# Sums of weight tiles and weight blocks as adding transfers from GpSimd's queue, in a delta-rule attention followed by a gated FFN

## The chip, the cores and the metric

The kernel runs on one core of one Trainium2 chip. The metric is the device time of one execution in microseconds (us), as a median over runs. A profile is one execution taken by the hardware profiler; it times every instruction on the five engines: PE (TensorE, the matrix engine; PEld is its weight load), DVE (VectorE), ACT (ScalarE), POOL (GpSimd) and SP (SyncE), and the transfers of the 16 DMA engines.

## The reference

The inputs are q, k and v of 4 batches x 8 heads x 768 steps x 48 columns and beta, all float32, and three weight matrices (gate and val 384 x 1536, out 1536 x 384), which are float64, and a gain of 384.

```python
k_n = k / (norm(k) + 1e-06)
for t in range(S):                      # state: 48 x 48 per batch and head, from zero
    y[:, :, t] = einsum('bhd,bhde->bhe', q[:, :, t], state)
    v_old = einsum('bhde,bhd->bhe', state, kt)
    state = state + bt * einsum('bhd,bhe->bhde', kt, vt - v_old)
x = y.transpose(0, 2, 1, 3).reshape(3072, 384)
xn = x / sqrt(mean(x * x) + 1e-06) * rms_g
g = xn @ w_gate
out = (g * sigmoid(g) * (xn @ w_val)) @ w_out
```

## The kernel before, in words

The sequence is cut into 12 chunks of 64 steps (NCH = 12). Of each chunk, `prep` builds what does not depend on the state: the transposed keys, the products of keys with keys (L532), and by a recursion of DVE steps (L693, a product, and L699, a sum, 15 of each per chunk) the inverse of a triangular 64 x 64 matrix per head, assembled from 32-step halves through DRAM (`dkk`, `dx`, `dxt`) and two merges on PE (L775, L799). For chunks 0 and 1 the products with beta at its start (L646, L671, L676) run on DVE, for later ones on POOL. `recur` then applies the state: `on_state` (L840) multiplies the transposed keys and queries with it, L886 and L900 give the corrected values and the output, `ku` (L1019) and a sum on DVE (L1028) update the state. Keys and state are padded from 48 to 64 rows per head (`DP`), so that two heads lie in the two halves of the 128 partitions; pairs of 64-row halves and 64-column halves of PE are used side by side. The output of a chunk (256 tokens x 384) is normed, transposed and scaled into `xf` (or `xp1` for chunk 1).

The FFN of chunks 0 and 1 (`ffn_plain`) multiplies directly: 12 column blocks of 128, each an `up` (L1064: gate and val), silu on ACT (L1071), a product on DVE (L1072) and a `down` (L1046). Its first half uses blocks 0 to 5 (half 0 of the weights) of chunk 0 and then chunk 1, its second half blocks 6 to 11 (half 1). The FFN of chunks 2 to 11 (`ffn`) uses fewer block products: 15 products per half of the weights (L1157) of sums of the input blocks with sums of the weight blocks, and a similar scheme in `down` (L1214). A `more_` product is added into `tmp` on DVE (L1167), another is copied by ACT (L1169).

The weights come as 64-bit floats in 18 tiles of 768 KB, in the order of `weights`: per half, pairs of gate and val for three input column groups, with the three tiles of `w_out` in between (tiles 4, 7, 8 and 13, 16, 17). A tile is loaded into one of three `raw` buffers (parts of `more`) and converted with integer steps: ACT makes the scaled high word (L460), DVE shifts it (L448), masks it into a scratch tile `cc` (L451) and multiplies the low word in (L456), and the sum of both is written into `w_in` or `wo_sb` (L480). `cc` is one of two buffers, `tmp` for even tiles and a part of `more` for odd ones. Tiles 0 to 2 are summed on PE (L472, L473), all others on DVE.

`factors(h)` makes the sums of weight blocks of half h for `ffn`: six into `extra[h]`, which lies where the raw buffers and the odd `cc` were, and two in place in `w_in`, once the plain FFN has read that half (the key `wuse`). They are 13 DVE instructions per half (L1120, L1122), each 128 x 512. `out_factors` (L1193) does the like for `w_out`.

No engine decides at run time: a list scheduler in the file (`Plan`) takes each step's engine, estimated duration, dependencies and priority, with due times for some transfers (`after`), simulates 60 rounds with a random shake from a seed, and emits the best order found, which every engine then follows in its own queue. Padding matmuls (`filler`, L1312) are put into planned gaps of PE in the first 70 us of the plan.

Of the kernel before, what the change touches and what calls it, by code (L numbers as in the profile page):

```python
# [59 lines left out]
class Plan:  # L60
# [150 lines left out]
    def run(self, free, filler=None, until=0.0):  # L211
        self.first_priorities()
        best = None
        self.ends = []
        rng = random.Random(19)
        for k in range(ROUNDS):
            order = self.forward([t for t, _ in free], until if filler else 0.0)
            if order is None:
                break
            self.ends.append(self.end)  # L220
            if best is None or self.end < best[0]:
                best = self.end, [(op, op.start) for op in order]
            self.backward()
            for op in self.ops:
                op.key += SHAKE * (k % 3) * rng.uniform(-1.0, 1.0)
        self.end = best[0]
        pe = 0.0
        free = list(free)
        for op, s in best[1]:
            op.start = s  # L230
            for g in op.acquire:
                if g.t is None:
                    g.t = free.pop(0)[1]
            if filler and op.eng == "PE":
# [12 lines left out]
def kernel(  # L247
# [113 lines left out]
    def dma(dst, src, prio, r=(), w=(), work=0.3, dur=0.5, eng="SP", after=0.0):  # L361
        queue = nc.scalar if eng == "ACT" else nc.sync
        op = P.add(eng, dur, lambda: queue.dma_start(out=dst, in_=src), prio, r, w, lat=0.7)
        op.dma, op.work, op.ready = True, work, after

    PERIOD = 51.0

    def due(c, lead):
# [51 lines left out]
    def weights():  # L420
        todo = []
        for half_ in range(2):
            c0 = half_ * WCOL

            for i_ in range(3):
                for side, (key, w) in enumerate((("wg", moe_w_gate), ("wv", moe_w_val))):
                    c1 = c0 + 256 * i_
                    src = w.rearrange("(t p) c -> p t c", p=128)[:, :, c1 : c1 + 256]
                    todo.append((w_in[:, side, half_, i_:9:3], src, [(key, half_, i_)]))
                if i_:  # L430
                    for f in ((6 * half_,) if i_ == 1 else (6 * half_ + 2, 6 * half_ + 4)):
                        src = moe_w_out[f * 128 : f * 128 + 256, :].rearrange("(a p) c -> p a c", a=2)
                        z = spot(f)
                        todo.append((wo_sb[:, z : z + 2], src, [("wo", f), ("wo", f + 1)]))
        for n, (dst, src, keys) in enumerate(todo):
            pr = (30 if n < 9 else CV2) + 0.2 * n
            i, a = n % NRAW, n % NCV
            parts = dst.shape[1]
            rdst = raw[i].rearrange("p (a c) -> p a c", a=parts)
            dma(rdst, src, (0.1 if n == 0 else 3 + 2 * n), w=[("raw", i)], dur=0.7, work=3.06, after=(0.8, 5.0, 16.7, 24.5, 24.5, 33.3, 50.0)[n] if n < 7 else 53.0)  # L440
            words = raw[i].bitcast(U32).rearrange("p (a n two) -> p a n two", a=parts, two=2)
            low, high = words[:, :, :, 0], words[:, :, :, 1]
            u = dst.bitcast(U32)
            cc = cvb[a].rearrange("p (a n) -> p a n", a=parts)
            cvk = [("o", 1)] if a else [("tmp", 1), ("tmp", 2)]

            def s2(u=u):
                nc.vector.tensor_scalar(out=u, in0=u, scalar1=3, scalar2=None, op0=ALU.logical_shift_left)  # L448

            def s4(u=u, cc=cc):  # L450
                nc.vector.tensor_scalar(  # L451
                    out=cc.bitcast(U32), in0=u, scalar1=0xFF800000, scalar2=None, op0=ALU.bitwise_and
                )

            def s5(low=low, cc=cc, by=2.0**-52):
                nc.vector.scalar_tensor_tensor(out=cc, in0=low, scalar=by, in1=cc, op0=ALU.mult, op1=ALU.mult)  # L456

            P.add("ACT", 0.84, lambda high=high, dst=dst: nc.scalar.activation(out=dst, in_=high.bitcast(FP32), func=ACTF.Prelu, scale=2.0**-112, alpha=2.0**32), pr, r=[("raw", i)], w=[("cvw", n)])  # L460
            P.add("DVE", 0.66, s2, pr, w=[("cvw", n)])
            P.add("DVE", 0.66, s4, pr, r=[("cvw", n)], w=cvk)
            P.add("DVE", 1.0, s5, pr, r=[("raw", i)], w=cvk)
            done = []
            if n < NPE:
                for x_ in range(2):
                    ps = Group()
                    cut = slice(2 * x_, 2 + x_)
                    m = 512 - 256 * x_

                    def s6(ps=ps, dst=dst[:, cut], cc=cc[:, cut], m=m):
                        nc.tensor.matmul(ps.t[:, 0:m], ident, dst, start=True, stop=False)  # L472
                        nc.tensor.matmul(ps.t[:, 0:m], ident, cc, start=False, stop=True)  # L473

                    P.add("PE", 0.0035 * m, s6, pr, r=cvk + [("cvw", n), "ident"], w=[("cvp", n, x_)], ps=ps, size=8)
                    done.append(("cv", n, x_))
                    P.add("ACT", A(m), lambda dst=dst[:, cut], ps=ps, m=m: nc.scalar.copy(dst, ps.t[:, 0:m].rearrange("p (a n) -> p a n", n=256)), pr, r=[("cvp", n, x_), ("cvw", n)], w=[done[-1]], last=ps)
            else:
                done.append(("cv", n))
                P.add("DVE", 0.97, lambda dst=dst, cc=cc: nc.vector.tensor_tensor(out=dst, in0=dst, in1=cc, op=ALU.add), pr, r=cvk, w=[("cvw", n), done[-1]])  # L480
            for key in keys:
                ready.setdefault(key, []).extend(done)

# [3 lines left out]
    def load(c, what):  # L487
        t0 = c * C
        pk, pq, pv = ((-5, 1, 12), (5, 29, 36))[c] if c < 2 else (due(c, 150), due(c, 99), due(c, 70))
        for key, t, src, pr in (("k2", k2[c % NK], k, pk), ("q2", q2, q, pq)):  # L490
            for g in range(2):
                if key[0] not in what:
                    continue
                dst = t[64 * g : 64 * g + 64, :, 0:D]
                s = src.rearrange("b (y g) t e -> g t (b y) e", g=2)[g, t0 : t0 + C]
                dma(dst, s, pr, w=[(key, c % NK if key == "k2" else 0, g)], dur=0.7, work=1.02, eng="ACT" if c == 0 and g and key == "k2" else "SP", after=((0.8, 0.0, 0.0), (7.8, 20.8, 0.0))[c]["kqv".index(key[0])] if c < 2 else 60.3)
        if "v" in what:
            for bb in range(2):
                s = v[2 * bb : 2 * bb + 2, :, t0 : t0 + C, :].rearrange("p h t e -> t (p h) e")
                dma(vt[64 * bb : 64 * bb + 64], s, pv, w=[("v", bb)], dur=0.85, work=1.02, after=(30.4, 34.6)[c] if c < 2 else 60.0)  # L500

    def turn(src, dst, keys, r, pr, split):

# [314 lines left out]
    def recur(c):  # L818
# [11 lines left out]
        if c:  # L830
# [276 lines left out]
    )  # L1107
    PLACE = ((0, 0), (2, 1), (0, 1), (1, 1), (1, 0), (2, 0))

    def factors(h):  # L1110

        w_ = lambda i, k_: w_in[:, :, h, 3 * k_ + i]
# [4 lines left out]
        def two(out_, a, b_, op, neg=False, over=False):  # L1117
# [12 lines left out]
        two(e(0), w_(1, 0), w_(0, 0), sub)  # L1130
        two(e(1), e(0), w_(0, 1), sub, neg=True)
        two(e(0), e(0), w_(0, 2), add)
        two(e(2), w_(0, 0), w_(0, 2), sub)
        two(e(2), e(2), w_(2, 0), sub)
        two(e(3), w_(2, 1), w_(2, 2), sub)
        two(e(4), e(3), w_(0, 1), sub)
        two(e(3), w_(1, 1), e(3), sub)
        two(e(5), w_(0, 1), w_(2, 0), add)
        two(w_(2, 1), w_(2, 1), w_(1, 1), sub, over=True)
        two(w_(2, 1), w_(2, 1), w_(2, 0), sub, over=True)  # L1140
        two(w_(0, 0), w_(1, 2), e(0), sub, over=True)
        two(w_(0, 0), w_(0, 0), e(3), sub, over=True)

    def ffn(c, start):
        n = 0
        for h in range(2):
            ps = [Group() for _ in range(3)]
            for m, ((kind, slot), xs, b_, begin, o, more_, end) in enumerate(PRODUCTS):
# [197 lines left out]
```

## Time and profile before

| | |
|---|---|
| median of 3 runs | 718.07 us (716.91 to 720.38) |
| the profiled execution | 720.75 us, span 719.0 us from the first to the last instruction, PE clock 0.993 |
| busy in the span | PE 701.6, PEld 652.8, DVE 553.8, ACT 314.3, POOL 152.1 us |
| DMA | 54.68 MB, mean 76 GB/s; nearly all on the queue that serves SP, none issued by POOL |
| L480, the tile sums on DVE | 15 instructions, 128x768 |
| L1122 and L1120, factor sums on DVE | 24 and 2 instructions, 128x512, 0.68 to 0.89 us each |
| L840 and L1019, state and its update | 22 and 11 groups of 64 matrix instructions |

Lines of the profile give the start in us, the busy time in us, the engine, the line of the kernel, the operation, what is written and read with its shape, how often, and in square brackets the idle time of the engine just before it and what ended it. A busy PE is not always useful, since L1312 is filler. A fp32 matmul is recorded as two instructions. A group that is slow beside another engine's work shows as a spread between the least and the greatest duration. Landing is the time from the issue of a transfer to its completion.

### The profile page before, as it was taken

To read this page: it belongs to the slowest core of one execution; us is meant where nothing else is said; L and a number is where in the kernel's file an instruction comes from. 1 tells how busy PE (TensorE), PEld (TensorE's weight loads), DVE (VectorE), ACT (ScalarE), POOL (GpSimd) and SP (SyncE) were. 2 spreads that over 40 slices of the span, in tenths; PEclk is the share of its full clock that TensorE was granted. 3 is DMA by queue.
4 is the path that set the end of the run, shared out by engine and by line. 5 is a ranking of instruction groups with operands and counts; after the bars stand their busy time and mean duration, and the time that the engine had idled before them with its cause. 6 is when DMAs were issued, how large, how long until landed. Compare 5 with 4: busy or idle time off the path is not lost.

```text
span 719.0 us, 23540 instructions
## 1 busy us (share of the span) xinstructions
PE 701.6 (98%) x10178; PEld 652.8 (91%) x10178; DVE 553.8 (77%) x1128; ACT 314.3 (44%) x732; POOL 152.1 (21%) x150
## 2 busy tenths in 40 slices
PE   8988999999999999999999999999999999999997
PEld 7787877777799999998999999999999999999997
DVE  4898989998967958946967967975968958847473
ACT  5514544232345436354345255355355354344331
POOL 4200307004314132203213303203203221000000
PEclk9998999999999999999999999999999999999999
DMA  8867698141154261242234253253152061040000
GB/s 172 208 127 169 141 251 233 23 66 43 35 87 80 39 111 27 46 73 59 57 58 78 44 95 55 40 86 65 38 106 48 13 115 28 13 65 2 23 1 23
DMA packets 210071, 54.68 MB, mean 76 GB/s; under 512 B 199216, under 2 KB 202288, under 8 KB 209968
## 3 DMA queue, kind: packets, MB, share of 16 engines
q1 hardware_dynamic: 205120, 52.26, 36.4%
q8 instruction: 80, 1.31, 0.8%
q10 hardware_dynamic: 4848, 0.92, 0.7%
q14 instruction: 23, 0.19, 0.1%
HBM read 40.83 MB, written 12.32 MB: 74 GB/s over the span
## 4 chain that ended last, share of the span: by engine, by line
PE 79%; DVE 12%; DMA 4%; issue 2%; SPq 1%; POOL 1%; ACT 1%; ACTq 0%; DVEq 0%; POOLq 0%
PE bank L1157 36%; PE bank L1214 19%; PE bank L1064 6%; PE bank L1046 3%; PE bank L532 3%; PE bank L840 2%; PE bank L509 2%; DVE acc L699 2%; DMA more<-in_moe_w_gate_dram 2%; PE bank L799 2%; PE bank L886 1%; PE bank L1019 1%; PE bank L900 1%; DVE w_in L480 1%; DVE acc L693 1%
## 5 line engine op out<-in xcount | busy, mean ns | idle before, releaser
L1167 DVE TENSOR_TENSOR tmp<-tmp,bank 128x512 f32<-128x512 f32 x180 | 122.0, 685 | 85.9 <-PE bank L1157 75.9
L1157 PE MATMUL bank<-xf,w_in 128*128 128x128 f32 x1440 | 181.5, 277 | 0.2 <-DVE tmp L1167 0.2
L1157 PEld LDWEIGHTS bank<-xf,w_in 128*128 128x128 f32 x1440 | 169.8, 192 | 2.6 <-DVE tmp L1167 0.6
L1157 PE MATMUL bank<-xf,more 128*128 128x128 f32 x960 | 124.7, 277 | 0.0
L1157 PEld LDWEIGHTS bank<-xf,more 128*128 128x128 f32 x960 | 115.6, 192 | 1.7 <-DVE tmp L1167 0.4
L1169 ACT COPY tmp<-bank 128x512 f32<-128x512 f32 x120 | 68.5, 584 | 82.1 <-PE bank L1157 57.2
L699 DVE TENSOR_REDUCE acc<-acc 128x30 f32<-128x90 f32 (+4 forms) x180 | 85.1, 473 | 6.2
L1173 ACT ACTIVATE tmp<-tmp 128x256 f32<-128x256 f32 x120 | 49.7, 417 | 87.9 <-DVE tmp L1167 87.5
L693 DVE TENSOR_TENSOR acc<-acc,at 128x60 f32<-128x60 f32 (+4 forms) x180 | 63.4, 352 | 8.7 <-POOL at L676 5.9
L1214 PE MATMUL bank<-wo_sb,hf 128*128 128x192 f32 x360 | 63.8, 328 | 0.0
L1174 DVE TENSOR_TENSOR hf<-tmp 128x256 f32<-128x256 f32 x120 | 51.8, 443 | 13.0 <-ACT tmp L1173 11.7
L1214 PEld LDWEIGHTS bank<-wo_sb,hf 128*128 128x128 f32 x360 | 58.2, 190 | 0.3
L646 POOL TENSOR_TENSOR at<-at,beta_b 128x1024 f32<-128x1024 f32 x10 | 25.6, 2555 | 146.1 <-DMA at<-dkk 146.1
L554 POOL TENSOR_TENSOR knrm<-ksum,half 128x16 f32<-128x16 f32 x12 | 35.9, 2991 | 33.4 <-DVE ksum L553 33.4
L720 POOL COPY acc<-acc 128x128 f32<-128x128 f32 x40 | 17.1, 458 | 116.9 <-DVE acc L699 116.1
L1312 PE MATMUL bank<-ident 128*128 128x128 f32 x298 | 40.3, 296 | 1.4 <-POOL ident masks.py:199 1.4
L1312 PEld LDWEIGHTS bank<-ident 128*128 128x128 f32 x298 | 38.1, 209 | 2.5 <-POOL ident masks.py:199 1.4
L1046 PE MATMUL bank<-wo_sb,hf 128*128 128x384 f32 x96 | 34.3, 491 | 0.3 <-DVE r L854 0.3
L1064 PE MATMUL bank<-xf,w_in 128*128 128x256 f32 x144 | 33.6, 382 | 0.0
L1064 PE MATMUL bank<-xp,w_in 128*128 128x256 f32 x144 | 33.4, 383 | 0.0
L1064 PEld LDWEIGHTS bank<-xf,w_in 128*128 128x128 f32 x144 | 26.8, 190 | 4.9
L1064 PEld LDWEIGHTS bank<-xp,w_in 128*128 128x128 f32 x144 | 26.7, 190 | 4.4 <-issue 0.2
(164 smaller groups left out, 1047.9 us busy)
## 6 DMA issues: line engine op xcount, KB each, us to landing
at<-dkk SPq DMA_DIRECT2D x23, 256.0 KB, 4.0
q<-in_q_dram SPq DMA_DIRECT2D x24, 192.0 KB, 3.8
more<-in_moe_w_gate_dram SPq DMA_DIRECT2D x6, 768.0 KB, 6.0
more<-in_moe_w_val_dram SPq DMA_DIRECT2D x6, 768.0 KB, 7.2
more<-in_moe_w_out_dram SPq DMA_DIRECT2D x6, 768.0 KB, 8.4
vt<-in_v_dram SPq DMA_DIRECT2D x24, 192.0 KB, 4.2
out_dram<-tmp SPq DMA_DIRECT2D x48, 96.0 KB, 2.2
k<-in_k_dram SPq DMA_DIRECT2D x23, 192.0 KB, 4.2
```

The lines of the kernel that those rows point to most:

```text
L554: P.add("POOL", 2.95, lambda: nc.gpsimd.tensor_tensor(out=knrm[i2], in0=ksum[i2], in1=half, op=ALU.pow), pn, r=[("ksum", i2), "half"], w=[ ...
L693: nc.vector.tensor_tensor(out=acc[:, 1:3, 0:n, j + 2 : W].rearrange("p a i t -> p i a t"), in0=acc[:, old, 0:n, j : j + 2, None].to_broadc ...
L699: nc.vector.tensor_reduce(out=acc[:, new, 0:n, j + 2 : W], in_=acc[:, lo : lo + 3, 0:n, j + 2 : W].rearrange("p a i t -> p i t a"), axis=A ...
L1046: nc.tensor.matmul(po[p].t[:, 0:DM], hf[:, spot(f), 128 * p : 128 * p + 128], wo_sb[:, spot(f)], start=(f == f0), stop=(f == f1 - 1), skip ...
L1064: nc.tensor.matmul(ps.t[:, TOK * side : TOK * side + TOK], w_in[:, side, h_, 3 * t + i_, n : n + 128], x_[:, 2 * t : 2 * t + 2].rearrange( ...
L1157: nc.tensor.matmul(g.t[:, 128 * z : 128 * z + 128], fac[:, side, 128 * f : 128 * f + 128], xf[:, xs], start=(begin and z == 0), stop=False ...
L1167: P.add("DVE", V(512), lambda t=t, g=g: nc.vector.tensor_tensor(out=t, in0=t, in1=g.t, op=ALU.add), -1, r=[g], w=[tk], last=g)
L1169: P.add("ACT", A(512), lambda t=t, g=g: nc.scalar.copy(t, g.t), -1, r=[g], w=[tk], last=g)
L1173: P.add("ACT", A(256), lambda t=t: nc.scalar.activation(out=t[:, 0:256], in_=t[:, 0:256], func=ACTF.Silu), -1, w=[tk])
L1174: P.add("DVE", V(256), lambda t=t, f0=f0, p=p: nc.vector.tensor_tensor(out=hf[:, spot(f0) : spot(f0) + 2, 128 * p : 128 * p + 128], in0=t[ ...
L1214: nc.tensor.matmul(g.t[:, 0:192], a_[:, f], b_[:, f], start=(begin and f == 0), stop=(f == 5), skip_group_check=True)
L1312: nc.tensor.matmul(warm[:, 0:128], ident, ident)
```

## The change

Five things are edited.

1. A helper `gather` issues a transfer on POOL's queue whose data are added to what the destination holds (`accum_op`). The planner reckons with 1.2 us on POOL and 1.5 us of latency for it.
2. The last step of a weight tile's conversion: tiles 6 to 17 (n >= NDV) add `cc` into the tile with one such transfer; tiles 3 to 5 keep DVE's sum.
3. `factors` is rebuilt from `build`: ACT copies the first block (with a negated sign where needed), one or two transfers add the others, and where the sum has to be negated ACT multiplies by -1 at the end. Per half these are 8 copies, 5 signs and 15 transfers in place of 13 DVE sums. The products of `ffn` depend on all eight keys of their half.
4. `on_state` uses 48 of the 64 rows of each head, `ku` writes 48 of 64 rows from 48 columns of K.
5. The planner's seed goes from 19 to 38, and due times of loads move: K of chunk 1 from 7.8 to 5.0, K and Q of later chunks from 60.3 to 61.8, V of chunks 0 and 1 from 30.4 and 34.6 to 28.5 and 32.8.

```diff
-        rng = random.Random(19)
+        rng = random.Random(38)
...
+    def gather(dst, src, prio, r, w, work):
+
+        op = P.add("POOL", GDUR, lambda: nc.gpsimd.dma_start(out=dst, in_=src, accum_op=ALU.add), prio, r, w, lat=GLAT)
+        op.dma, op.work, op.port = True, work, False
+
+    GDUR, GLAT, NDV, NDF = 1.2, 1.5, 6, 0
...
-                P.add("DVE", 0.97, lambda dst=dst, cc=cc: nc.vector.tensor_tensor(out=dst, in0=dst, in1=cc, op=ALU.add), pr, r=cvk, w=[("cvw", n), done[-1]])
+                if n < NDV:
+                    P.add("DVE", 0.97, lambda dst=dst, cc=cc: nc.vector.tensor_tensor(out=dst, in0=dst, in1=cc, op=ALU.add), pr, r=cvk, w=[("cvw", n), done[-1]])
+                else:
+                    gather(dst, cc, pr, r=cvk, w=[("cvw", n), done[-1]], work=1.5)
...
-                                rows, u, n = slice(64 * d, 64 * d + 64), 4 * bb + x_, 96 * x_ + 48 * g
+                                rows, u, n = slice(64 * d, 64 * d + D), 4 * bb + x_, 96 * x_ + 48 * g
...
-                                nc.tensor.matmul(pss[g].t[64 * d : 64 * d + 64, n : n + 48], kn[rows, x_], u_[rows, x_])
+                                nc.tensor.matmul(pss[g].t[64 * d : 64 * d + D, n : n + D], kn[rows, x_, 0:D], u_[rows, x_])
...
+        def build(out_, first, minus, more_, neg, over=False):
+
+            p_ = (170.0, 0.0)[h] if over else pr
+            k_ = ("fac", h, len(fackeys[h]))
+            r = list(fackeys[h][0:6]) if over else wk
+            w = [k_] + ([("wuse", h), ("wx", h)] if over else exkeys[h])
+            fackeys[h].append(k_)
+            P.add("ACT", A(512), lambda: nc.scalar.mul(out_, first, -1.0) if minus else nc.scalar.copy(out_, first), p_, r=r, w=w)
+            for t in more_:
+                gather(out_, t, p_, r=r, w=[k_], work=1.0)
+            if neg:
+                P.add("ACT", A(512), lambda: nc.scalar.mul(out_, out_, -1.0), p_, r=r, w=[k_])
...
+            build(e(0), w_(0, 0), True, (w_(1, 0), w_(0, 2)), False)
+            build(e(3), w_(2, 1), True, (w_(1, 1), w_(2, 2)), False)
+            build(e(1), w_(0, 0), True, (w_(1, 0), w_(0, 1)), True)
+            build(e(2), w_(0, 0), True, (w_(0, 2), w_(2, 0)), True)
+            build(e(4), w_(2, 1), True, (w_(2, 2), w_(0, 1)), True)
+            build(e(5), w_(0, 1), False, (w_(2, 0),), False)
+            build(w_(2, 1), w_(2, 1), True, (w_(1, 1), w_(2, 0)), True, over=True)
+            build(w_(0, 0), w_(1, 2), True, (e(0), e(3)), True, over=True)
...
-                P.add("PE", 0.9, mm, start + 0.95 * n, r=["xc", ("xp", 0), ("xp", 1), ("wx", h)], w=[g] + first, ps=g, size=16)
+                P.add("PE", 0.9, mm, start + 0.95 * n, r=["xc", ("xp", 0), ("xp", 1), ("wx", h)] + fackeys[h], w=[g] + first, ps=g, size=16)
```

More of the change, by code (lines that the diff above doesn't have):

```diff
@@ L495, in load @@
                 s = src.rearrange("b (y g) t e -> g t (b y) e", g=2)[g, t0 : t0 + C]
-                dma(dst, s, pr, w=[(key, c % NK if key == "k2" else 0, g)], dur=0.7, work=1.02, eng="ACT" if c == 0 and g and key == "k2" else "SP", after=((0.8, 0.0, 0.0), (7.8, 20.8, 0.0))[c]["kqv".index(key[0])] if c < 2 else 60.3)
+                dma(dst, s, pr, w=[(key, c % NK if key == "k2" else 0, g)], dur=0.7, work=1.02, eng="ACT" if c == 0 and g and key == "k2" else "SP", after=((0.8, 0.0, 0.0), (5.0, 20.8, 0.0))[c]["kqv".index(key[0])] if c < 2 else 61.8)
         if "v" in what:
@@ L499, in load @@
                 s = v[2 * bb : 2 * bb + 2, :, t0 : t0 + C, :].rearrange("p h t e -> t (p h) e")
-                dma(vt[64 * bb : 64 * bb + 64], s, pv, w=[("v", bb)], dur=0.85, work=1.02, after=(30.4, 34.6)[c] if c < 2 else 60.0)
+                dma(vt[64 * bb : 64 * bb + 64], s, pv, w=[("v", bb)], dur=0.85, work=1.02, after=(28.5, 32.8)[c] if c < 2 else 60.0)
     def turn(src, dst, keys, r, pr, split):
@@ L1108 @@
     PLACE = ((0, 0), (2, 1), (0, 1), (1, 1), (1, 0), (2, 0))
+    fackeys = [[], []]
     def factors(h):
@@ L1127, in two @@
                 P.add("DVE", V(512), fn, pr, r=wk, w=exkeys[h] + [("ex", h)])
-        add, sub = ALU.add, ALU.subtract
[L1130 to L1142, printed above, removed]
+        def build(out_, first, minus, more_, neg, over=False):
[9 more added lines that the diff above has]
+                P.add("ACT", A(512), lambda: nc.scalar.mul(out_, out_, -1.0), p_, r=r, w=[k_])
@@ new lines, in factors @@
+        add, sub = ALU.add, ALU.subtract
+        if h < NDF:
+            two(e(0), w_(1, 0), w_(0, 0), sub)
+            two(e(1), e(0), w_(0, 1), sub, neg=True)
+            two(e(0), e(0), w_(0, 2), add)
+            two(e(2), w_(0, 0), w_(0, 2), sub)
+            two(e(2), e(2), w_(2, 0), sub)
+            two(e(3), w_(2, 1), w_(2, 2), sub)
+            two(e(4), e(3), w_(0, 1), sub)
+            two(e(3), w_(1, 1), e(3), sub)
+            two(e(5), w_(0, 1), w_(2, 0), add)
+            two(w_(2, 1), w_(2, 1), w_(1, 1), sub, over=True)
+            two(w_(2, 1), w_(2, 1), w_(2, 0), sub, over=True)
+            two(w_(0, 0), w_(1, 2), e(0), sub, over=True)
+            two(w_(0, 0), w_(0, 0), e(3), sub, over=True)
+        else:
+            build(e(0), w_(0, 0), True, (w_(1, 0), w_(0, 2)), False)
[6 more added lines that the diff above has]
+            build(w_(0, 0), w_(1, 2), True, (e(0), e(3)), True, over=True)
```

## The prediction

> **What bounds the kernel now.** I read the page's slices first, then busy times by stage, then PE's waits, then the order of time around each step that the diff touches.
>
> ```profile
> PE   8988999999999999999999999999999999999997
> DVE  4898989998967958946967967975968958847473
> DMA  8867698141154261242234253253152061040000
> ```
>
> PE is full almost from the start, but a busy PE is not yet a useful one: until 74.5 us much of it is the filler of L1312 (298 matmuls in all, 40.3 us). The first block matmul (L1064) starts at 74.54 us. So I cut the span there, at 128 us (weights converted but for two tiles) and at 199.7 us (the first L1157, chunk 2's FFN). Columns: length, then busy time (and instructions) of PE, PEld, DVE, ACT, POOL, then PE's clock, the DMA share and GB/s.
>
> ```profile
> 0.00:74.50 74.50, 66.36 (x1000) 59.39 (x1001) 58.57 (x124) 34.19 (x75) 13.62 (x19) 0.93 0.74 166
> 74.50:128.00 53.50, 50.38 (x861) 39.84 (x860) 50.23 (x70) 26.58 (x57) 19.23 (x11) 1.00 0.81 207
> 128.00:199.70 71.70, 71.70 (x634) 55.20 (x635) 65.96 (x132) 21.20 (x51) 17.14 (x17) 1.00 0.23 42
> 199.70:650.00 450.30, 448.46 (x7080) 434.30 (x7079) 341.56 (x733) 210.03 (x497) 101.16 (x103) 1.00 0.34 61
> ```
>
> From 74.5 us PE runs real work without a break: 3.1 us idle up to 128, none to 199.7, 1.8 in the next 450. DVE is nearly as full before 199.7 (94 and 92%), and that is where the diff takes work away, but DVE's load costs time only where PE waits for it. PE's waits in 74 to 130 us (total, times, longest):
>
> ```profile
> PE bank L509 <- DVE hf L1072: 1.2, 1, 1.2
> PE bank L509 <- issue: 0.6, 1, 0.6
> ...
> PE bank L1046 <- DVE r L854: 0.3, 1, 0.3
> ```
>
> The five waits listed there sum to 3.2 us, 1.5 of them for DVE. That is the ceiling for any relief of DVE behind 74.5 us. Ahead of it the chain to chunk 0's FFN is one of latencies, with one place where DVE is late:
>
> ```profile
> 58.46 1.08 PE L775 MATMUL bank<-m1bd,kk 128*32 128x64 f32 x32 [2.86 <-DVE m1bd L764]
> ```
>
> L764's copy was ready to run at 54.5 us (L751's matmuls start at 53.41 and last 1.1), and DVE came to it at 57.48, after recursion steps of chunk 1.
>
> **The change, part by part.**
>
> *Sums of 12 weight tiles (L480, n from 6 on) leave DVE.* One clean sum takes 0.957 us; some are stretched:
>
> ```profile
> L480 DVE TENSOR_TENSOR w_in<-w_in,more x4: 953/958/960, 74.2 to 145.3; 128x768 f32<-128x768 f32 x4
> L480 DVE TENSOR_TENSOR w_in<-w_in,tmp x4: 949/1532/2996, 81.2 to 118.1; 128x768 f32<-128x768 f32 x4
> ```
>
> L480 is busy 16.3 us after 74.5; less the end of tile 5's sum (0.6) that is 15.7 us off DVE: 12 x 0.957 = 11.5 clean, and 4.2 that was waiting beside POOL (the 3.00 us sum starts at 118.12, while POOL runs L646 from 117.13 to 120.30). Worth on the path: at most the 3.1 us of PE's idle time, at least nothing. DVE's share of the waits is 1.5; some of the rest is order. I take 2.0 us gained.
>
> What comes instead: 12 issues on POOL's queue, 384 KB each. Landing, bounded by these rows (KB, us from issue to landing):
>
> ```profile
> at<-dkk SPq DMA_DIRECT2D x23, 256.0 KB, 4.0
> more<-in_moe_w_gate_dram SPq DMA_DIRECT2D x6, 768.0 KB, 6.0
> more<-in_moe_w_out_dram SPq DMA_DIRECT2D x6, 768.0 KB, 8.4
> ```
>
> So a converted tile is ready some 4 to 8 us after its product, not 1 us; I take 5 (384 KB is nearest to the first row). Hidden if the tile is not needed yet. Tiles 9 to 17 feed matmuls from 141 us on, and all but two were summed by 126.7 us: 14 us of cover. Tiles 6 to 8 were summed by 83.3, 78.2 and 87.9 us; the matmuls that end the first block's first half run from 95.8 to 108: 8 us of cover, the thinnest. Tiles 15 and 17 (summed at 146.3 and 149.7) are needed at 157.7 (chunk 0, blocks 10 and 11) and about 164. The scratch tile cc is held until the transfer has read it; with two of them the mask step of tile n+2 (L451) waits for landing n, about 2 us beyond the 3 us of conversion between. DVE has other work for that gap. I cost it at nothing; without cover it is 12 x 2 = 24 us of DVE, against 15.7 freed.
>
> DMA engines: 207 GB/s at a share of 0.81 is 256 GB/s when full, so 384 KB takes 1.5 us, 3.1 if the destination's read counts as much. Twelve are 18 to 37 us, against 10.2 us idle in 74.5 to 128 (19% of 53.5) and 55 in 128 to 199.7. Loads of late tiles slip by some 8 us into the idle stretch: inside the cover above.
>
> *26 factor sums (L1120, L1122) leave DVE, 26 copies and signs go to ACT, 30 transfers to POOL.* DVE loses 26 x 0.69 = 17.9 us between 149.9 and 200.7, where PE waits for nothing: no gain. ACT gains 26 x 0.586 (the row of L1169, the same size) = 15.2 us; it was busy 21.2 of 71.7. POOL: an issue lies between 0.37 us (SP's for a 768 KB load) and 2.92 (L554, POOL's dearest small instruction); I take 1.3 (L676, a 128x512 sum on POOL), close to the 1.2 that the new plan reckons with. From 143 to 200 us that is about 29 issues, 38 us, beside 17.8 us of present work in 57 us: POOL goes from a third to nearly full, and its queue is in order. It holds chunk 3's decay steps:
>
> ```profile
> 167.31 3.40 POOL L646 TENSOR_TENSOR at<-at,beta_b 128x1024 f32<-128x1024 f32 x1 [22.81 <-DMA at<-dkk]
> ...
> 174.04 1.29 POOL L676 TENSOR_TENSOR at<-at,acc 128x512 f32<-128x512 f32 x1
> ```
>
> ```profile
> 175.37 0.22 DVE L693 TENSOR_TENSOR acc<-acc,at 128x60 f32<-128x60 f32 x1 [2.64 <-POOL at L676]
> ```
>
> DVE already waits 2.64 us for them, and what follows (recursion to 197.7, stores, loads, L775 at 214) has little slack: the last x2bd load is issued from 211.2 to 213.1 and takes 2.7 to land (median of x2bd), so about 215.8, and L799 reads it at 216.7. The second transfer into a factor also has to wait for the first to land (4 us), and a queue blocked there blocks L646. Interleaved over eight factors this hides. I charge 1.0 us; ends 0 and 10.
>
> Deadlines: half 0's eight factors must land by 199.7 us; starting about 147, 15 issues of 1.3 and a last landing take 25 us, so 27 us to spare. Half 1's two in-place factors start when the last block matmul has read w_in (194.6) and take copy 0.6, two transfers of 5.3, a second issue 1.3, sign 0.6: 207.7. The first product of half 1 runs near 218.6 (the 121st L1157): 11 us to spare. ACT's sign waits with PSUM copies queued behind it, so a late landing shows first there.
>
> The port: L480's 2996 against 957 ns shows DVE and POOL delaying each other. The Trainium skill, "SBUF — State Buffer", section "Who interferes with whom", goes further and against this change: descriptors written by GpSimd are shut out while DVE holds the shared port pair, and the other way round. By it each of the 12 issues could cost DVE a further 1 us or so, an estimate that would eat the 11.5 us freed and end the sum 2 us higher; no run here shows it yet.
>
> *48 columns of K.* on_state and ku are 33 groups of 64 instructions, 1.08 us each (202.59 to 203.67 for one). The 64x64 group of L532 takes 1.09 for 64 columns moved instead of 48, and L751 with 32x32 tiles takes 1.04 (86.68 to 87.72): the shape hardly matters, so the cost is per instruction. Gain at most 33 x 0.04 = 1.3 us; I take 0.3. The other end, that 48 rows no longer run four at a time, would be tens of microseconds; the tiles still start at 0 and 64, so I give it 3%.
>
> *Seed and due times.* The whole order is drawn again. Up to 74.5 us nothing else changes, so the first block may start up to 3 us earlier (the 2.86 us above) or as much later. I take 0, ends -3 and +3. Behind 199.7 PE is full: up to 1 us either way.
>
> **Sum.** 0 - 2.0 + 1.0 - 0.3 + 0 = -1.3 us. The profiled execution took 720.75 us (span 719.0), 2.7 above the median of 718.07; I set the difference against the median: 716.8.
>
> **Rivals.**
> *The new order starts the block phase early* and DVE's relief closes all gaps: -3 - 3.1 and up to -1.3: about 712.5. For it: the 2.86 us wait, and a DVE that has 94% load in 74.5 to 128. Against: nothing taken off DVE lies ahead of 74.5 us.
> *POOL's queue becomes the wait* (slower): transfers that wait for landings stand ahead of L646 of chunk 3, and L799 at 216.7 us comes late by as much. It decides from about 1 us of delay, the slack above, and passes 0.5% at one landing and some more (5 us); two landings are 8 us, less 1 of slack: 725. At 2.92 us an issue POOL would need 85 + 18 us in 57 and the loss would be over 30 us; I give that 0.03 of the 0.24 below.
> *Nothing of it matters:* all moved work was hidden and stays hidden; neither the waits shrink nor new ones come: 718.
>
> **How the numbers follow.** About 0.5% (3.6 us) is what a measurement tells from no change. Forecast: 0.32. Nothing matters: 0.10. Early start: 0.31. POOL's queue, or late weights in the same place: 0.24. Concurrency lost: 0.03, which the range leaves out. The range reaches from 709.5 (early start with all small gains, 3 us below its own value) to 725 (two landings). Of the forecast's chance 0.03 lies below 714.5, so faster is 0.34, same 0.39, slower 0.27. The likeliest case alone holds 714.5 to 720.
>
> **What would show it.** Right: L1064 starts within 3 us of 74.5; PE's idle time from there to 128 falls below 2 us; DVE's share in 128 to 199.7 falls to about 70%; L840 and L1019 stay at 1.08 us a group. Wrong: PE waits for POOL, for a landing into w_in or more, or for ACT's sign between 140 and 220 us; L646 of chunk 3 starting later than 170; POOL issues well over 1.3 us; L1157 beginning more than 3 us away from 199.7.

## The result, and the profile after

The changed kernel takes 741.87 us (median of 4 runs, 740.23 to 744.44) where the kernel before takes 718.84: a ratio of 1.0326, with an interval of 1.0305 to 1.0346. That is 23 us slower, where 1.3 us faster was forecast, and outside the range of 709.5 to 725. The profiled execution took 740.23 us (span 738.5).

In the changed kernel L1064 has become L1073, L1157 L1191, L886 L895, L900 L909, L1019 L1028, L693 L702, L646, L671 and L676 L655, L680 and L685, L451 L457; the new transfers are issued at L368, the factor copies at L1147. The page's slices and DMA queues after:

```profile
PE   8998998997599899999999999999999999999997
...
PEclk9999999999699999999999999999999999999999
DMA  7956999799986316125216234243253042030000
...
q1 hardware_dynamic: 205120, 52.26, 35.7%
q0 software_dynamic: 11680, 12.59, 11.1%
```

One dip stands in PE's row (7 and 5 in the tenth and eleventh slice, 166 to 203 us) and in the clock's (6), and the DMA row is 7 to 9 from 74 us up to it. q0 is the new queue: 12.59 MB in 11680 packets of 1.08 KB, for 11.1% of 16 engines' span, which is 82 us of all 16 engines (0.111 x 738.5) or 112 ns a packet. The same cuts as before (length; PE, PEld, DVE, ACT, POOL; clock, DMA share, GB/s; a share above 1 is packets that overlap):

```profile
74.50:128.00 53.50, 49.64 (x850) 38.48 (x849) 30.48 (x53) 23.40 (x52) 24.53 (x18) 1.00 1.02 216
128.00:199.70 71.70, 58.27 (x446) 45.19 (x445) 36.36 (x74) 23.78 (x51) 44.71 (x39) 0.90 1.07 173
199.70:650.00 450.30, 446.85 (x6967) 428.53 (x6967) 350.84 (x750) 212.35 (x508) 113.69 (x113) 1.00 0.36 64
```

DVE is relieved as the diff says (from 94 and 92% to 57 and 51%), and PE does not gain: it stands idle for 13.4 us in 128 to 199.7, where it had no idle time, and 3.9 against 3.1 in the stretch before. The DMA share there went from 0.23 to 1.07. Over the span, PE's idle time grew by 15.1 us (32.5 against 17.4) and its busy time by 4.4, together the 19.5 us between the spans. PE's waits, most costly first:

```profile
PE bank L895 <- DMA mt<-dx: 10.6, 1, 10.6
PE bank L784 <- DVE m1bd L773: 3.3, 1, 3.3
PE bank L909 <- DVE u L934: 2.0, 1, 2.0
```

L784's wait, ahead of the first block, stood in the kernel before too (2.9 us). One wait carries most of what is new: before chunk 2's corrected values, for `mt`, a piece of the triangular inverse that comes back from DRAM. The instructions around it on PE, each with the idle time in front:

```profile
178.77 2.86 PE L1073 MATMUL bank<-xp,w_in 128*128 128x256 f32 x12
192.21 2.28 PE L895 MATMUL bank<-r,mt 64*64 64x48 f32 x64 [10.58 <-DMA mt<-dx]
194.42 2.93 PE L1073 MATMUL bank<-xp,w_in 128*128 128x256 f32 x6
```

After the wait the clock is down too (0.50 granted in 190 to 195 us, 0.68 in 195 to 200): the L895 group takes 2.28 us, where the kernel before's took 1.15, and six matmuls of L1073 2.93 us instead of 1.46. The chain that ended last, in order of time (start, length, what):

```profile
154.15 14.94 DMA dx<-acc
169.13 0.30 SPq L363
...
182.60 9.37 DMA mt<-dx
191.96 0.25 issue
192.21 2.28 PE bank L895 x64
```

The way from `dx` to `mt` is the same short set of transfers in all kernels. SP's issues of it, first before, then after:

```profile
145.56 1.26 SPq L363 DMA_DIRECT2D dx<-acc  x2
151.06 3.90 SPq L363 DMA_DIRECT2D mt<-dx  x8
```

```profile
150.90 1.49 SPq L363 DMA_DIRECT2D dx<-acc  x1
154.15 2.66 SPq L363 DMA_DIRECT2D dx<-acc  x1
173.32 10.71 SPq L363 DMA_DIRECT2D mt<-dx  x8
```

Before, the last `mt` is issued at 155.0 and lands 2 us later, at 157, and PE needs it at 175.4 (the first L886 with `mt`): 18 us of cover. After, the chain starts 5.3 us later; from the first `dx` issue to the first `mt` issue it takes 22.4 us instead of 5.5 (+16.9); the eight `mt` issues take 9.3 us to the last landing's start, not 3.9 (+5.4); the last landing takes 9.4, not 2 (+7.4). That is 35 us of delay on 18 of cover, and 17 us is what PE's L895 is late (192.2 against 175.4). The first FFN product of chunk 2 (L1191) starts at 213.33, 13.6 us later than before.

Why the small transfers are slow, from the DMA queues and the issues (KB, median us to landing) in 140 to 200 us, before and after:

```profile
q1 hardware_dynamic: 13152, 2.49, 23.1%
...
dx<-acc SPq DMA_DIRECT2D x2, 128.0 KB, 3.0
mt<-dx SPq DMA_DIRECT2D x8, 32.0 KB, 2.0
...
m1bd<-dxt SPq DMA_DIRECT2D x2, 64.0 KB, 2.6
```

```profile
q0 software_dynamic: 7613, 8.12, 89.6%
q1 hardware_dynamic: 11279, 2.93, 28.2%
...
more<-w_in POOLq DMA_DIRECT2D x22, 256.0 KB, 11.5
...
dx<-acc SPq DMA_DIRECT2D x2, 128.0 KB, 10.7
mt<-dx SPq DMA_DIRECT2D x8, 32.0 KB, 6.5
...
m1bd<-dxt SPq DMA_DIRECT2D x2, 64.0 KB, 14.1
```

The adding transfers alone fill 89.6% of the 16 engines for 60 us; three kinds of transfer on which chunk 2's chain runs land 3 to 5 times later.

### The profile page after: what moved, and what is told of

It is laid out like the page before. It is cut to its first block, busy times and chain, and to the rows that moved or that the text cites. A ratio compares the mean times of both kernels' runs of the same rounds, so it can differ in the third digit from the quotient of the medians.

```text
span 738.5 us, 23610 instructions
## 1 busy us (share of the span) xinstructions
PE 706.0 (96%) x10176; PEld 654.1 (89%) x10176; DVE 524.8 (71%) x1090; ACT 324.7 (44%) x758; POOL 199.7 (27%) x192
## 3 DMA queue, kind: packets, MB, share of 16 engines
q1 hardware_dynamic: 205120, 52.26, 35.7%
q0 software_dynamic: 11680, 12.59, 11.1%
## 4 chain that ended last, share of the span: by engine, by line
PE 67%; DMA 11%; DVE 10%; SPq 5%; issue 4%; POOL 2%; ACT 1%; ACTq 0%; DVEq 0%; POOLq 0%
PE bank L1191 33%; PE bank L1248 18%; SPq L363 5%; PE bank L518 2%; DVE acc L708 2%; PE bank L849 2%; PE bank L541 2%; DMA dx<-acc 2%; DMA more<-in_moe_w_gate_dram 2%; DVE acc L702 2%; DMA mt<-dx 2%; PE bank L1073 1%; PE bank L909 1%; PE bank L895 1%; DMA wsum<-dx 1%
## 5 line engine op out<-in xcount | busy, mean ns | idle before, releaser
L1191 PE MATMUL bank<-xf,w_in 128*128 128x128 f32 x1440 | 180.8, 277 | 0.0
L1191 PEld LDWEIGHTS bank<-xf,w_in 128*128 128x128 f32 x1440 | 169.8, 192 | 2.4 <-issue 0.4
L1191 PE MATMUL bank<-xf,more 128*128 128x128 f32 x960 | 124.6, 277 | 0.0
L1191 PEld LDWEIGHTS bank<-xf,more 128*128 128x128 f32 x960 | 115.2, 192 | 1.8 <-issue 0.4
L702 DVE TENSOR_TENSOR acc<-acc,at 128x60 f32<-128x60 f32 (+4 forms) x180 | 64.3, 357 | 18.9 <-POOL at L685 16.1
L1208 DVE TENSOR_TENSOR hf<-tmp 128x256 f32<-128x256 f32 x120 | 54.6, 464 | 16.1 <-ACT tmp L1207 15.2
L655 POOL TENSOR_TENSOR at<-at,beta_b 128x1024 f32<-128x1024 f32 x10 | 27.4, 2742 | 121.5 <-DMA at<-dkk 99.9
L729 POOL COPY acc<-acc 128x128 f32<-128x128 f32 x40 | 16.8, 521 | 105.3 <-DVE acc L708 104.6
L563 POOL TENSOR_TENSOR knrm<-ksum,half 128x16 f32<-128x16 f32 x12 | 38.5, 3204 | 17.9 <-DVE ksum L562 17.8
L1346 PE MATMUL bank<-ident 128*128 128x128 f32 x296 | 38.8, 291 | 1.4 <-POOL ident masks.py:199 1.4
L1346 PEld LDWEIGHTS bank<-ident 128*128 128x128 f32 x296 | 36.5, 203 | 2.4 <-POOL ident masks.py:199 1.4
L1073 PE MATMUL bank<-xp,w_in 128*128 128x256 f32 x144 | 34.9, 395 | 1.6 <-ACT xp L999 1.1
L368 POOL DMA_DIRECT2D more<-w_in x22 | 34.8, 3217 | 1.2 <-ACT more L1147 1.2
L1073 PEld LDWEIGHTS bank<-xp,w_in 128*128 128x128 f32 x144 | 27.5, 196 | 7.2 <-ACT xp L999 1.7
L1073 PE MATMUL bank<-xf,w_in 128*128 128x256 f32 x144 | 33.7, 383 | 0.0
## 6 DMA issues: line engine op xcount, KB each, us to landing
more<-w_in POOLq DMA_DIRECT2D x22, 256.0 KB, 11.5
```

Source lines behind the costliest of these rows:

```text
L563: P.add("POOL", 2.95, lambda: nc.gpsimd.tensor_tensor(out=knrm[i2], in0=ksum[i2], in1=half, op=ALU.pow), pn, r=[("ksum", i2), "half"], w=[ ...
L702: nc.vector.tensor_tensor(out=acc[:, 1:3, 0:n, j + 2 : W].rearrange("p a i t -> p i a t"), in0=acc[:, old, 0:n, j : j + 2, None].to_broadc ...
L1073: nc.tensor.matmul(ps.t[:, TOK * side : TOK * side + TOK], w_in[:, side, h_, 3 * t + i_, n : n + 128], x_[:, 2 * t : 2 * t + 2].rearrange( ...
L1191: nc.tensor.matmul(g.t[:, 128 * z : 128 * z + 128], fac[:, side, 128 * f : 128 * f + 128], xf[:, xs], start=(begin and z == 0), stop=False ...
L1208: P.add("DVE", V(256), lambda t=t, f0=f0, p=p: nc.vector.tensor_tensor(out=hf[:, spot(f0) : spot(f0) + 2, 128 * p : 128 * p + 128], in0=t[ ...
L1346: nc.tensor.matmul(warm[:, 0:128], ident, ident)
```

## The experiments

The theory: the adding transfers keep the DMA engines busy, and the chain's small transfers stand in the way. Rivals: POOL's queue (30 issues and waits in front of chunk 3's steps); the new order itself; the waits for landings and signs (PE shows no wait for a landing into `w_in` or `more`, nor for a sign). Each ratio below is to runs of the kernel before that were taken beside that experiment; their median lay between 718.15 and 720.49 us.

**All transfers thin.** The changed kernel in its own order, each adding transfer with only the first 16 columns of every run. All issues, waits, semaphores, copies and signs stay; 0.75 of 12.59 MB is moved.

```diff
-        op = P.add("POOL", GDUR, lambda: nc.gpsimd.dma_start(out=dst, in_=src, accum_op=ALU.add), prio, r, w, lat=GLAT)
+        op = P.add("POOL", GDUR, lambda: nc.gpsimd.dma_start(out=dst[:, :, 0:16], in_=src[:, :, 0:16], accum_op=ALU.add), prio, r, w, lat=GLAT)
```

> The changed kernel in its own order, but each adding transfer moves only the first 16 columns of each run (64 bytes instead of 1 KB or more), so the sums of tiles and factors are left out for the other columns; issues, waits and landings stay in place. Theory T (traffic: the added bytes fill the 16 DMA engines from 140 to 200 us, so chunk 2's small transfers dx and mt land late and PE waits 10.6 us at L895): L895's wait falls under 2 us, the first L1191 starts at 198 to 203 us instead of 213.3, and the time is 718 to 725. Theory Q (GpSimd's in-order queue and the chain of landings cause the wait): the transfers still wait for one another, L895 stays late by over 6 us, 734 to 742. Theory O (the new order alone): 738 to 742.

723.56 us, ratio 1.008 (1.0061 to 1.0098) to 718.15. Some 18 of the 23 us are gone. The profiled execution took 719.97 us, the fastest of the four, so the 5.4 us that are left in the median do not show in it. Its queue and stretches:

```profile
q0 software_dynamic: 12320, 0.75, 3.2%
```

```profile
74.50:128.00 53.50, 52.18 (x861) 40.31 (x860) 34.77 (x66) 23.95 (x53) 25.60 (x18) 1.00 0.84 179
128.00:199.70 71.70, 69.81 (x531) 54.61 (x530) 48.52 (x98) 35.05 (x79) 59.46 (x52) 1.00 0.53 66
```

It has even more packets on q0 (12320), but a packet takes 30 ns and not 112, `dx` lands in 3.5 us and `mt` in 2.1, and L895 begins at 174.9 without a wait. POOL is busier here than in the changed kernel (59.5 of 71.7 us), and that costs next to nothing:

```profile
175.50 0.22 DVE L702 TENSOR_TENSOR acc<-acc,at 128x60 f32<-128x60 f32 x1 [4.39 <-POOL at L685]
```

DVE waits for POOL 4.39 us instead of 2.64, and goes on at 175.50, where the kernel before did at 175.37. So the number of issues and packets and POOL's queue are not what those 18 us are; the time for which the packets hold the engines is. The adding transfers' own landings fall with it (those into `more` from 11.5 to 5.1 us).

**Only tiles, only factors, neither.** These leave one kind of sum on DVE; the planner draws a new order for each. The diff is that of tiles only; factors only has 18, 0 as the last two numbers, neither 18, 2.

```diff
-    GDUR, GLAT, NDV, NDF = 1.2, 1.5, 6, 0
+    GDUR, GLAT, NDV, NDF = 1.2, 1.5, 6, 2
```

> The changed kernel with the factors summed by DVE as before (12 tile transfers stay, the 30 factor transfers go; the plan draws its order anew). T: between 140 and 200 us only the last tiles' transfers are left, so 718 to 726; the loads of tiles run slower in 75 to 128 but are hidden. Q: GpSimd's queue is free again from 155 us on, 718 to 726 as well. O: 736 or more.

> The changed kernel with all tile sums from tile 3 on made by DVE and the factors by 30 transfers (order drawn anew). T and Q: the factor transfers still stand beside dx and mt of chunk 2 in 150 to 200 us, so most of the loss stays: 730 to 742. O: 736 or more. If the tiles' transfers were the cause: under 724.

> The changed kernel with no adding transfer at all: seed, due times and 48 columns of K alone. T and Q: 714 to 721 (the ku groups take 0.87 us instead of 1.08, 11 of them, 2.3 us less; the order within 3 us either way). O: 736 or more.

Tiles only 733.24 us (1.0202, 1.0179 to 1.0225), factors only 728.89 (1.0146, 1.0126 to 1.0166), neither 726.31 (1.011, 1.0095 to 1.0125). The last one has no adding transfer at all, and is 8 us slower: its first block matmul starts at 83.06 us instead of 74.54. The copy of `m1bd` (L773), for which PE waited 2.86 us before, now stands on DVE behind eleven of the fifteen steps of chunk 1's recursion, where four stood ahead of it before (it started at 57.48 us there):

```profile
65.15 0.85 DVE L773 COPY m1bd<-bank 32x256 f32<-32x256 f32 x2
```

None of the three came out as the theory had it. They differ by their drawn orders as much as by what they were made for, and cannot split the loss. For that the order has to be kept, as in the next two.

**Thin factors, thin tiles.** The order of the changed kernel, one kind of transfer cut to 16 columns. The diff is that of thin factors; thin tiles asks for work == 1.5 instead.

```diff
-        op = P.add("POOL", GDUR, lambda: nc.gpsimd.dma_start(out=dst, in_=src, accum_op=ALU.add), prio, r, w, lat=GLAT)
+        op = P.add("POOL", GDUR, lambda: nc.gpsimd.dma_start(out=dst[:, :, 0:16] if work == 1.0 else dst, in_=src[:, :, 0:16] if work == 1.0 else src, accum_op=ALU.add), prio, r, w, lat=GLAT)
```

> The changed kernel in its own order; only the 30 factor transfers are cut to 16 columns of each run (the factors' other columns stay unsummed), the 12 tile transfers move all their bytes. e1_thin gave 723.6 with both cut. If the bytes of the factors are what holds chunk 2's dx and mt: 723 to 727, L895 waits under 3 us. If the last tiles' bytes do it: 735 or more. If both burst together: in between.

> The changed kernel in its own order; only the 12 tile transfers are cut to 16 columns of each run, the 30 factor transfers move all their bytes. Factors as the cause: 736 to 742, dx of chunk 2 lands in over 7 us (14.9 in the changed kernel) and L895 waits over 6 us. Tiles as the cause: under 728.

Thin factors 735.06 us (1.0186, 1.0135 to 1.0237), thin tiles 731.54 (1.0131, 1.0079 to 1.0183). The first is what I expected of the tiles as the cause, the second lies between the prices of both causes. Against all thin (723.56), full tiles cost 11.5 us by the medians and full factors 8.0, and the changed kernel is 18.3 above. But all thin was run at another time, and by the ratios, each to its own runs of the kernel before, it is 7.6 and 3.7 us (each within some 4) and 17.7 for both. So the tiles' cost is clear of the noise, that of the factors alone is less certain, and whether the two add up or make more together is not settled. They work in different places.

Full tiles make the whole stretch from 74.5 to 128 us slip. Its DMA share was 0.81 before; it is 0.84 all thin, 0.91 with thin tiles, and 1.02 to 1.03 with full ones. What slips is the weights' stream (the last mask step, L451 or L457, starts at 147.1 us before, 146.5 all thin, 148.2 with thin tiles, 154.4 in the changed kernel, 156.0 with thin factors) and, with it, chunk 2's way to its inverse, which shares SP's queue and the engines: POOL's first product of chunk 2 (L646, L655) starts at 117.1 us before, 115.8 all thin, 117.4 with thin tiles, 122.1 in the changed kernel, 123.5 with thin factors. In the changed kernel it waits for a transfer of 256 KB on SP's queue:

```profile
122.13 2.36 POOL L655 TENSOR_TENSOR at<-at,beta_b 128x1024 f32<-128x1024 f32 x1 [4.05 <-DMA at<-dkk]
```

The first `dx` follows, in the same order of kernels, at 145.6, 145.3, 146.9, 150.9 and 152.3. With thin factors PE idles 4.8, 5.3 and 6.4 us in the three stretches from 74.5 to 650 (all thin: 1.3, 1.9 and 2.4).

Full factors crowd the chain itself: with thin tiles q0 takes 84.9% of the engines in 140 to 200 us, `mt` lands in 5.0, `x2bd` in 6.5 and `m1bd` in 6.8 us (2.1 each, all thin). The single long wait that I expected here did not come: the chain starts early enough, and the loss is spread behind 199.7 us, where PE idles 9.6 us:

```profile
PE bank L909 <- DVE u L934: 3.9, 2, 3.2
PE bank L1191 <- ACT tmp L1203: 2.4, 1, 2.4
...
PE bank L518 <- POOL k L630: 1.5, 1, 1.5
```

Only together do a late start and slow transfers outrun the 18 us of cover at one place. And the POOL rival is not nothing once the transfers are full: with thin factors POOL's queue is on the chain to L909, where PE waits 4.40 us.

```profile
185.44 0.22 DVE L702 TENSOR_TENSOR acc<-acc,at 128x60 f32<-128x60 f32 x1 [8.07 <-POOL at L685]
```

There chunk 3's L655 starts at 161.55 (152.00 all thin, with as many transfers in the queue), so POOL's queue seems to pass on the slip of the tiles rather than to make it.

**The same transfers without the addition.** Same bytes, issues and waits; the data of the copy replace those of the destination.

```diff
-        op = P.add("POOL", GDUR, lambda: nc.gpsimd.dma_start(out=dst, in_=src, accum_op=ALU.add), prio, r, w, lat=GLAT)
+        op = P.add("POOL", GDUR, lambda: nc.gpsimd.dma_start(out=dst, in_=src), prio, r, w, lat=GLAT)
```

> The changed kernel in its own order with the same transfers as plain copies: the source overwrites the destination and nothing is added, so sums are left out. If the cost lies in the addition (the destination is read too, 112 ns a packet of about 1 KB in the changed kernel): packets of GpSimd's queue take 40 to 70 ns, the queue's share falls from 11.1% to 4 to 7%, and the time falls to 724 to 732. If any transfer of that size costs as much: 738 to 742.

725.81 us, ratio 1.0081 (1.0047 to 1.0114).

```profile
q0 software_dynamic: 3584, 12.59, 5.7%
```

I had expected shorter packets (40 to 70 ns); they are fewer and longer instead. As copies the same bytes go in 3584 packets of 3.5 KB that take 184 ns each: 41 us of all 16 engines (0.057 x 723.7), half of the 82. An issue is cheaper as well (0.72 us for a factor). So 16 to 18 of the 23 us (by the medians, by the ratios) belong to the addition. This run takes both away, engine time and issue time, and does not tell them apart; the thin run does, for there the issues are as dear as in the changed kernel (POOL is busy 34.8 us with the 22 issues into `more` in both).

The copies fill the engines as well while they run (a share of 1.05 in 150 to 176 us), and chunk 2's small transfers are late here too, in 140 to 200 us:

```profile
dx<-acc SPq DMA_DIRECT2D x2, 128.0 KB, 6.4
mt<-dx SPq DMA_DIRECT2D x8, 32.0 KB, 5.7
```

But the first `dx` is issued at 148.9 us and the last `mt` at 167.3, which lands in at most 9.4, and L895 begins at 177.3 without a wait for it. So copies slow the chain too, though less (`m1bd` lands in 6.2 us and not in 14.1), and here the cover just hides it.

**The planner told what the transfers cost.** The work that the plan counts on the DMA engines goes to the measured 2.6 and 1.75 us, an issue to 1.3.

```diff
-    GDUR, GLAT, NDV, NDF = 1.2, 1.5, 6, 0
+    GDUR, GLAT, NDV, NDF = 1.3, 1.5, 6, 0
...
-                    gather(dst, cc, pr, r=cvk, w=[("cvw", n), done[-1]], work=1.5)
+                    gather(dst, cc, pr, r=cvk, w=[("cvw", n), done[-1]], work=2.6)
...
-                gather(out_, t, p_, r=r, w=[k_], work=1.0)
+                gather(out_, t, p_, r=r, w=[k_], work=1.75)
```

> The changed kernel with the planner told what the changed kernel's trace showed: 2.6 us of the DMA engines for a tile's transfer and 1.75 for a factor's, not 1.5 and 1.0, and 1.3 us of GpSimd's queue (order drawn anew). If the loss is a plan made with transfers that are too cheap: chunk 2's dx and mt move ahead of the factors and the time falls to 718 to 730. If the DMA engines lack the time whatever the order: 733 to 745.

760.80 us, ratio 1.0544 (1.049 to 1.0598): worse, against what was expected. The order drawn has a wait of 21.9 us ahead of the first block, which now starts at 96.58 us:

```profile
PE bank L784 <- ACT acc L660: 21.9, 1, 21.9
```

Whether another order could hide the transfers stays open; this one plan says nothing about all.

**The seed alone.** The kernel before with another draw.

```diff
-        rng = random.Random(19)
+        rng = random.Random(38)
```

> The kernel before with the planner's seed 38 in place of 19 and nothing else: the same work, drawn in another order. Theory: the draw of the order by itself is worth several microseconds, as in the kernel without any adding transfers (726.3, where the first block matmul began 8.5 us late), so 720 to 728 us, with the first block matmul between 75 and 84 us. Rival, the prediction's term: at most 3 us either way, 715 to 721 us, the first block matmul within 3 us of 74.5.

720.29 us, ratio 1.0015 (0.9993 to 1.0036), no measurable difference; the first block matmul starts at 76.38 us, 1.8 later, in a profiled execution that was the longest of ten (725.33 us). Both figures lie inside the theory's range and the rival's; the theory's several microseconds are not seen, the prediction's term holds here, and the seed by itself is no cause. The 8 us of the kernel with neither sum came with seed, due times and 48 columns, and which of them drew the bad order was not tried.

**48 columns in the update alone.** The kernel before, its order unchanged.

```diff
-                                nc.tensor.matmul(pss[g].t[64 * d : 64 * d + 64, n : n + 48], kn[rows, x_], u_[rows, x_])
+                                nc.tensor.matmul(pss[g].t[64 * d : 64 * d + D, n : n + D], kn[rows, x_, 0:D], u_[rows, x_])
```

> The kernel before in its own order, with one edit: the update of the state (ku) takes 48 columns of K and writes 48 rows; the adding transfers, the seed, the due times and on_state's 64 rows stay as before. Theory: the 11 groups of ku fall from 1.08 to about 0.87 us, which is 2.3 us of PE time in a stretch in which PE has no idle time, so the kernel takes 715 to 717 us where the kernel before takes 718 to 719 (ratio 0.997). Rival, the prediction's own term: the columns do not matter, at most 0.3 us is gained, ratio 1.000.

718.57 us against 720.49 of the kernel before, ratio 0.9974 (0.9957 to 0.9991): faster by some 1.9 us, and the one part of the change that was seen to pay. The groups of PE instructions before and here (busy us, mean ns):

```profile
L1019 PE MATMUL bank<-u,k 64*64 64x48 f32 x704 | 12.8, 220 | 0.0
```

```profile
L1019 PE MATMUL bank<-u,k 64*48 64x48 f32 x704 | 10.3, 207 | 0.0
```

2.5 us less PE time, most of it in 199.7 to 650 us, where PE hardly waits (1.8 us idle before). It is the fastest version that was run, by 0.26%.

## Why the prediction was wrong, step by step

**What bounds the kernel: right as far as it went.** PE had no idle time to give from 74.5 us on, and DVE's relief bought nothing: with all transfers thin DVE is down to 65 and 68% in the two stretches, and PE still idles 1.3 and 1.9 us there. The 2.0 us that I took as gained would have been at most the difference between 3.1 and 1.3 us, and the 1.9 us after 128 eat it.

**DMA engines, the step that failed.** I priced one tile transfer at 1.5 to 3.1 us of all engines, and the measured one lies between (384 KB is 3.1% of q0's bytes, and 3.1% of its 82 us is 2.6). But I multiplied it by 12 and stopped. The 30 factor transfers of 256 KB, 1.7 us each by the same share, are 51 us more, most of them in 154 to 200 us. I costed them on POOL, on ACT and by their landings, and never on the engines, with the 55 idle us of 128 to 199.7 on the page. The missing term fills that stretch; the 89.6% is it.

**"Loads of late tiles slip by some 8 us into the idle stretch: inside the cover": right in size, wrong in cover.** The last conversion's mask step came 7.3 us later (154.4 against 147.1). I measured the cover to the matmul that reads the tile. What slipped along with the tiles was the work that shares their queues and engines: chunk 2's `dkk` and `at`, its recursion, `dx` and `mt`, whose cover of 18 us I never looked up. And I let the transfers delay only each other and the loads; what a full set of engines does to a 32 KB transfer on a chain of five was not asked.

**Landing, taken as 5 us, ends 4 and 8: too low.** Tiles landed in 4.5 to 10.8 us, six of the first seven in over 9, and the factors in a burst in 11.5 (median). The row that I took as nearest (4.0 us) is a median of transfers most of which ran behind 128 us, where the engines were 0.23 to 0.34 busy. The mask steps did wait for landings that held `cc`, a cost that I had put at nothing, but for 2.7 us of DVE in all (0.3 all thin).

**POOL: the issue taken as 1.3 us was a little low, its effect small.** The 22 factor issues into `more` keep POOL busy for 34.8 us, 1.58 each. The rival "POOL's queue becomes the wait", decided by more than 1 us at L646, named the place that showed (L685, 9.20 us in the changed kernel), but with all issues kept and the bytes removed nothing was lost there. Chunk 3's L655 began at 159.66, well before the 170 that I had set as a sign. The sign that did show, a wait of PE for a landing between 140 and 220 us, I had tied to landings into `w_in` and `more`; it was one into `mt`.

**The page's rule on the port** would have cost DVE about 1 us for each tile issue. No run shows that. The six mask steps of the `wo_sb` tiles grew from 3.4 to 4.9 us in all, but the two that were stretched (1.53 and 1.18 us for 0.56) stand beside POOL's own product L655 (122.13 to 124.49) and its copies L729 (148.3 to 150.5), not beside an issue. One that lies inside the issues of two factors (153.68 to 156.27) kept its 0.56 us:

```profile
123.37 1.53 DVE L457 TENSOR_SCALAR more<-wo_sb 128x768 uint32<-128x768 uint32 x1
154.38 0.56 DVE L457 TENSOR_SCALAR more<-wo_sb 128x768 uint32<-128x768 uint32 x1 [0.92 <-DMA w_in<-more]
```

**48 columns, taken as 0.3, at most 1.3: mis-sized.** ku gained 1.9 us in the changed kernel (12.8 to 10.9 us busy; ten groups 0.21 us shorter each, one slower at a clock of 0.66 in 248 to 253 us) and 2.5 alone; on_state, which takes 48 rows instead of 64, gained nothing (220 ns a matmul in both). I compared the group of L532, which moves 64 columns where these move 48, and found them alike, which says nothing of the stationary side. In ku that has 48 columns instead of 64: its weight load fell from 135 to 122 ns and its matmul from 218 to 205. The Trainium skill, "TensorE: Matmul & The Clock Gate", section "LDWEIGHTS (loading the stationary operand)", says that the load's time goes by the columns and not by the rows; the two halves of this edit agree (on_state's load stays at 135 ns with 48 rows). So does L751 in the kernel before: with 32 stationary columns its load takes 108 ns, so a column is worth some 0.84 ns from 32 to 64. I had read only its group's 1.04 us, and why that group is not shorter is open.

**Order, taken as 0, ends -3 and +3: held in the changed kernel** (first block at 73.48 us against 74.54) and for the seed alone, but too narrow as a term: the kernel with neither sum was 8 us slower, with its first block 8.5 us late.

**The prices of the rivals.** Early start was added up wrongly: 718.07 - 3 - 3.1 is 712.0, or 710.7 with the 1.3, not 712.5; nothing in the result rests on it.

The sum as measured: some 18 us for the bytes of the transfers, and 5.4 between all thin and the kernel before, in which ku's gain of about 2 is already taken off; those 5.4 were not split among order, due times, issues, and ACT's copies and signs. Of the 0.27 for slower, 0.24 had been given to POOL's queue or late weights, whose price ended at 725; no rival named the engines' time.

## What to carry to other kernels

Work that is moved from an engine to the DMA queues has a price on the 16 DMA engines too: count every transfer that is added, bytes times the measured time of a byte, against the idle engine time of the very stretch, and not only against the engine that is relieved. Then look for the short chain of small transfers that runs in that stretch; its landings grow by a factor (3 to 5 here), while the 768 KB loads kept medians of 6.5 to 7.6 us (6.0 to 8.4 before). And when a planner redraws the order, test the parts with the order kept (cut the transfers thin, drop the addition), or the draws hide what is asked.

## What the runs showed of the hardware

- A transfer that adds to its destination costs the engines twice what a copy of the same bytes does: 1.08 KB packets of 112 ns (82 us of 16 engines for 12.59 MB, 153 GB/s) against 3.5 KB packets of 184 ns (41 us). Its issue on POOL took some 1.2 us at least for a factor (0.88 for a tile of `wo_sb`), the copy's 0.70 and 0.55.
- While q0 is full, 32 to 128 KB transfers of q1 land in 5.4 to 14.1 us (medians; 2.0 to 3.0 before), and SP's eight issues of `mt` take 0.9 to 1.7 us each (3.90 for eight, 0.5 each, before). With as many packets of 30 ns they do not. An explanation that fits: q1's packets take 21 ns each on average (0.357 x 738.5 us x 16 / 205120), and where each takes turns with one of 112 ns, a transfer of many small packets is slowed some 6 times. The Trainium skill, "DMA: Bandwidth & Descriptors", section "Queues, rings and completion order", says that an engine takes turns between queues packet by packet; that its packet is what the trace counts as one is not shown. It was argued from the averages; no run changed the packets' length at the same load, and the copies' packets of 184 ns did not make `mt` slower than those of 112 (5.7 against 6.5 us), so the explanation stays open.
- PE's granted clock was 0.73 in 180 to 190 us, 0.50 in 190 to 195 and 0.68 in 195 to 200, with PE busy for 1.6 of the 10 us before 190; the matmuls right behind the wait of 10.6 us took some 3 us more than in the kernel before (1.1 in L895, 1.5 in L1073, 0.4 in L909).
